# Four fused attention layers: the gates' loads moved a segment forward, a scale step, an update and two turns moved back on TensorE, and the first tiles' order rewritten

## The chip, the cores and the metric

The kernel runs on one NeuronCore of a Trainium2 chip. The metric is device time in microseconds (us) of one execution, as the median of several. Five engines work side by side, each through its own list of instructions in order: TensorE (PE in the profile; PEld is its weight loads), VectorE (DVE), ScalarE (ACT), GpSimd (POOL) and SyncE (SP, which here only issues DMAs).

## The reference

The input x has 2048 rows of 640 values; there are 32 heads of 20 values. Four layers follow each other, A, B, A, B, each on a normalized x and added to it, and both layers of a kind use the same weights.

```python
def _A_ref(x, wqkv, wo):                       # linear attention
    phi = lambda t: jnp.where(t > 0, t + 1, jnp.exp(t)) + 1e-6
    pq, pk = phi(q), phi(k)
    kv = jnp.einsum("bhsd,bhse->bhde", pk, v)
    z = jnp.einsum("bhsd->bhd", pk)
    num = jnp.einsum("bhqd,bhde->bhqe", pq, kv)
    den = jnp.einsum("bhqd,bhd->bhq", pq, z)[..., None] + 1e-6
    return (num / den) @ wo
def _B_ref(x, wq, wk, wv, wo, beta):           # 4 segments of 512 rows
    g = _sigmoid(beta).reshape(1, H, 1, 1)
    for s in range(N):
        p = _softmax(einsum("bhqd,bhkd->bhqk", qs, ks) * scale + mask)
        a_dot = jnp.einsum("bhqk,bhkd->bhqd", p, vs)
        num = jnp.einsum("bhld,bhde->bhle", phi(qs), M)
        den = jnp.einsum("bhld,bhd->bhl", phi(qs), z)[..., None] + 1e-6
        outs.append(g * num / den + (1.0 - g) * a_dot)
        M = M + jnp.einsum("bhld,bhle->bhde", phi(ks), vs)
        z = z + jnp.einsum("bhld->bhd", phi(ks))
x = x + _A_ref(_layernorm(x), ...); x = x + _B_ref(_layernorm(x), ...)   # twice
```

## The kernel before, in words

Rows are worked on in 4 segments of 512, each of 4 tiles of 128; the 640 columns are 5 chunks of 128. A value that TensorE multiplies is split in two fp16 parts, an upper half and a lower half (the rest), so that a product takes three matmuls per chunk: upper by upper, upper by lower, lower by upper. ACT writes upper halves, DVE lower ones, so almost each operand has an ACT step and a DVE step behind it.

**The opening** (`opening`, layer 1, up to about 260 us) prepares the eight weights while it computes the keys and queries of the first layer. `w_prep` prepares one: SP loads its five chunks into a stage (L239), DVE takes the largest magnitude of each (L243) and of these (L248), PE turns that column into a row with the identity (L252), DVE reduces the row (L254), PE spreads the one value to all partitions in a product with ones (L258: "the ones step"), DVE makes the scale of it (L261 to L264), ACT and DVE write the halves (L269, L270), and SP stores them (L275, wd). A turn (`turn`) is five transposes on PE (L329) whose result ACT and DVE copy as the halves of xT (L333, L334). Keys are products of xT with w_Ak (L406), then Exp and Relu on ACT (L418, L420), a sum on DVE (L421), and the halves pk (L556, L543). `memory` multiplies pk with xs, the normalized rows' halves (L487 on ACT, L488 on POOL, in `parts`), in products of L580, and DVE adds the results up (L602). At the end of segment 3 `merge` folds the memory with w_Av and w_Ao into one matrix wm: DVE takes reciprocals of the column sums (L646 to L648), scales the memory (L661), its halves are written (L663, L664), and PE multiplies them with w_Av (L682). `p_read` normalizes a tile of queries (pqi): POOL multiplies (L754, L760), DVE sums (rca, L757).

`gates` loads beta twice: as `gate`, 32 values on every partition (L205), and as `cg`, 8 columns on four rows, for which DVE first sets all to -10000 (L207) and SP issues four small loads (L209). Then ACT takes two Exps (L211, L212) and DVE adds one to each (L213, L214).

**The second phase** computes, layer by layer, queries times wm and the output (`a_head`, `a_second`), projects for the B layer (`b_project`), and runs B's attention beside it: scores (L993, L1034), maxima on DVE (L999), Exps on ACT (L1038), weighted sums (L1061). `b_project` also keeps the memory of layer B: for each of five chunks the keys' features pkT are turned by PE (L858), ACT copies the turn (pkt, L860), and `update` multiplies it with v (32 small matmuls, L868), which DVE adds to acc (L872 or L874). The last chunk's turn and update stand in `rest()`, which is woven with the next work, and its acc is masked to mem (L739), read by L457 a segment later.

**What sets the order.** PE's list is the order in which the code is written: parts of the work are generators, `weave` takes one step of the main one and a few of an auxiliary one in turn, and `pause(n)` lets n steps pass. On the other engines a scheduler orders the instructions by priority and readiness; `issue_after(x)` makes an instruction stand behind x, `high_priority` ahead of others. `busy(n)` issues n matmuls of the identity with itself (L320), whose result nobody reads.

## Time and profile before

| | |
|---|---|
| time, median of 3 runs | 1704.46 us (1704.25 to 1706.57) |
| profiled execution | 1704.55 us |
| its span, first to last instruction | 1702.8 us |
| mean granted TensorE clock | 0.992 |
| busy: PE, DVE, ACT, POOL | 96%, 75%, 58%, 30% of the span |

A row of the timeline gives the start, the time from there to the end of the last of its instructions, the engine, the line of the kernel, what is written and read, and how many instructions of a kind follow each other. In brackets stands how long the engine was idle ahead of it, and what ended that. SPq is SP's queue of DMA issues. A row of stretches gives, for each engine, the busy microseconds and the instructions, then the TensorE clock (1.00 is full speed), the share of time that the DMA engines were busy, and the rate.

### The profile page before, as it was taken

To read this page: it belongs to the slowest core of one execution; us is meant where nothing else is said; L and a number is where in the kernel's file an instruction comes from. 1 tells how busy PE (TensorE), PEld (TensorE's weight loads), DVE (VectorE), ACT (ScalarE), POOL (GpSimd) and SP (SyncE) were. 2 spreads that over 40 slices of the span, in tenths; PEclk is the share of its full clock that TensorE was granted. 3 is DMA by queue.
4 is the path that set the end of the run, shared out by engine and by line. 5 is a ranking of instruction groups with operands and counts; after the bars stand their busy time and mean duration, and the time that the engine had idled before them with its cause. 6 is when DMAs were issued, how large, how long until landed. Compare 5 with 4: busy or idle time off the path is not lost.

```text
span 1702.8 us, 37843 instructions
## 1 busy us (share of the span) xinstructions
PE 1637.9 (96%) x13788; PEld 1018.6 (60%) x13788; DVE 1272.3 (75%) x4015; ACT 994.2 (58%) x1888; POOL 505.9 (30%) x1046
## 2 busy tenths in 40 slices
PE   7999979999999999999999999999999999999998
PEld 5767757554465556556566777765546545645555
DVE  7888887487887788759874465847888978878773
ACT  6666533347756746667776454333675676666673
POOL 3442222013223322333452210310322332233452
PEclk9999989999999999999999999999999999999999
DMA  6424654421322331353211303423232323323432
GB/s 218 151 75 169 223 203 152 136 98 59 111 79 69 115 118 56 128 183 95 72 56 39 117 32 125 178 94 123 70 110 89 114 83 110 102 86 111 140 103 95
DMA packets 110372, 191.00 MB, mean 112 GB/s; under 512 B 14172, under 2 KB 69596, under 8 KB 107624
## 3 DMA queue, kind: packets, MB, share of 16 engines
q1 hardware_dynamic: 97704, 142.68, 25.9%
q0 software_dynamic: 3264, 24.91, 4.1%
q10 hardware_dynamic: 9216, 20.98, 3.2%
q8 instruction: 109, 1.79, 0.4%
q14 instruction: 79, 0.65, 0.1%
HBM read 109.32 MB, written 78.64 MB: 110 GB/s over the span
## 4 chain that ended last, share of the span: by engine, by line
PE 66%; DVE 17%; ACT 9%; issue 3%; DMA 3%; POOL 2%; SPq 0%; ACTq 0%; POOLq 0%; DVEq 0%
PE ps L406 25%; PE ps L391 13%; PE ps L1061 8%; PE ps L580 4%; PE ps L1034 4%; ACT pe L1038 3%; PE ps L993 3%; PE ps L329 3%; DVE ps L999 3%; PE ps L457 2%; PE ps L1074 1%; DVE e L421 1%; DVE wmx L243 1%; DVE split L270 1%; DVE xT L334 1%
## 5 line engine op out<-in xcount | busy, mean ns | idle before, releaser
L999 DVE CUSTOM_DVE_ANT_0 ps<-ps,maskw 128x512 f32<-128x512 f32 (+3 forms) x1024 | 472.0, 518 | 28.7 <-PE ps L993 25.9
L1038 ACT ACTIVATE pe<-ps,lsc 128x512 f32<-128x512 f32 x640 | 395.4, 696 | 63.0 <-PE ps L1034 59.8
L406 PEld LDWEIGHTS <-xT 128*128 128x128 f16 x2880 | 282.2, 99 | 115.0 <-issue 6.2
L1045 POOL TENSOR_SCALAR_AFFINE_SELECT pe<-pe 128x256 f32<-128x256 f32 (+1 forms) x640 | 233.4, 372 | 350.5 <-ACT pe L1038 342.7
L406 PEld LDWEIGHTS <-oT 128*128 128x128 f16 x1920 | 184.5, 98 | 84.7 <-issue 8.3
L1061 PE MATMUL ps<-pe,v 128*32 128x512 f32 (+3 forms) x2048 | 161.6, 436 | 8.8 <-DVE oT L334 1.9
L406 PE MATMUL ps<-wm,oT 128*128 128x320 f16 x960 | 141.3, 299 | 3.8 <-DVE rs L352 2.6
L406 PE MATMUL ps<-w_Bo,oT 128*128 128x320 f16 x960 | 141.5, 299 | 3.2 <-ACT oT L333 2.0
L406 PE MATMUL ps<-w_Ak,xT 128*128 128x320 f16 x960 | 140.6, 303 | 3.1 <-DVE xT L334 1.0
L406 PE MATMUL ps<-w_Bv,xT 128*128 128x320 f16 x960 | 142.3, 303 | 0.2
L391 PE MATMUL ps<-xT,w_Bq 128*128 128x512 f16 x600 | 140.9, 379 | 1.3 <-ACT pe L1038 0.8
L999 DVE DVE_READ_ACCUMULATOR2_ANT mg<- 128x1 f32 x1024 | 142.1, 139 | 0.1
L580 PE MATMUL ps<-pk,xs 128*128 128x321 f16 (+1 forms) x960 | 140.7, 304 | 1.1 <-DVE pk L543 0.7
L391 PE MATMUL ps<-xT,w_Bk 128*128 128x512 f16 x600 | 138.5, 379 | 1.2 <-ACT pe L1038 1.2
L406 PE MATMUL ps<-w_Aq,xT 128*128 128x320 f16 x960 | 137.6, 299 | 0.1
L993 PE MATMUL ps<-ks,qs 60*128 60x512 f16 (+3 forms) x1024 | 123.5, 297 | 7.6 <-ACT pe L1038 3.5
L580 PEld LDWEIGHTS <-xs 128*128 128x128 f16 x960 | 93.9, 99 | 41.0 <-issue 1.6
L421 DVE SCALAR_TENSOR_TENSOR e<-e,r 128x320 f32<-128x320 f32 x128 | 69.6, 544 | 53.6 <-ACT r L420 53.0
L1034 PE MATMUL ps<-qs,ks 62*128 62x512 f16 (+3 forms) x1024 | 105.6, 300 | 2.1 <-ACT pe L1038 1.1
L1061 PEld LDWEIGHTS ps<-pe,v 128*32 128x32 f32 x2048 | 65.4, 109 | 68.7 <-issue 40.9
L831 DVE SCALAR_TENSOR_TENSOR nat<-ps,nat 128x512 f16<-128x512 f32 x80 | 55.2, 690 | 62.6 <-ACT nat L830 62.3
L391 PEld LDWEIGHTS <-w_Bk 128*128 128x128 f16 x600 | 57.1, 98 | 66.5 <-issue 6.4
(202 smaller groups left out, 2359.6 us busy)
## 6 DMA issues: line engine op xcount, KB each, us to landing
x<-xn ACTq DMA_DIRECT2D x48, 320.0 KB
qs<-qd SPq DMA_DIRECT2D x128, 120.0 KB
ks<-kd SPq DMA_DIRECT2D x128, 120.0 KB
xo<-x SPq DMA_DIRECT2D x48, 320.0 KB
pqi<-pqd SPq DMA_DIRECT2D x32, 320.0 KB
qd<-nat SPq DMA_DIRECT2D x40, 256.0 KB
kd<-nat SPq DMA_DIRECT2D x40, 256.0 KB
x<-in_A_x SPq DMA_DIRECT2D x16, 320.0 KB
```

The costliest lines, as they stand in the source:

```text
L329: nc.tensor.transpose(pt[:, (c - c0) * P:(c - c0 + 1) * P], src[:, c * P:(c + 1) * P], self.ident)
L391: nc.tensor.matmul(p, w[:, c, a, t * P:(t + 1) * P], xT[:, c, b, :], start=k == 0, stop=k == 3 * C - 1)
L406: nc.tensor.matmul(p, xT[:, c, a, i * P:(i + 1) * P], w[:, c, b, n * HN:(n + 1) * HN], start=k == 0, stop=k == 3 * C - 1)
L421: nc.vector.scalar_tensor_tensor(e, e, 1.0, r, op0=OP.min, op1=OP.add)
L580: nc.tensor.matmul(p, xs[:, i, a, c * P:(c + 1) * P], pk[i][:, b, cols], start=i == 0 and a == b, stop=i == NT - 1 and a == 1)
L831: nc.vector.scalar_tensor_tensor(nat[:, 1], p, QK_SHIFT, nat[:, 0], op0=OP.mult, op1=OP.subtract)
L993: nc.tensor.matmul(bs[par][:, a:a + n], qs[r, p, i * P:(i + 1) * P], ks[r, p, :n], start=True, stop=True)
L999: nc.vector.tensor_tensor_reduce(bs[par][:, a:a + n], bs[par][:, a:a + n], self.maskw[:, SEG - n:], 1.0, NEG, OP.add, OP.max, G["mg"][:, p ...
L1034: nc.tensor.matmul(b[:, a:a + n], ks[r, p, j * P:(j + 1) * P], qs[r, p, j * P:], start=True, stop=True)
L1038: nc.scalar.activation(e, b, AF.Exp, scale=self.lsc)
L1045: nc.gpsimd.affine_select(d, d, pattern=pat, compare_op=OP.is_ge, fill=0.0, base=0, channel_multiplier=-1)
L1061: nc.tensor.matmul(G["pv"][32 * h4:32 * h4 + 32, j * P:], v[j][:, h * E1:h * E1 + 32], G.pop((p, par, j)), start=j == 0, stop=j == 2, skip ...
```

## The change

It has five parts.

1. `gates` is cut in two by a `yield`. Its loads and the setting of cg are taken in `late()`, an auxiliary step of segment 1, and the Exps and sums still in `last()`, in segment 3.
2. The ones step of weight A.v waits for 8 steps instead of 2.
3. The opening's first tiles: 11 identity products instead of 5 ahead of the first weight's maximum, 3 between its transpose and its ones step, 5 behind that in place of 3, and 4 behind the first two products. The first tile of keys takes its products in the order (0,0), (1,0), (0,1). `moments` is cut so that the second tile's shift (nb) stands behind six of the ten lower halves of w_Ak. The parts (xs) of a tile are queued behind the upper half of the next tile's turn.
4. In `p_read` the sum rca stands behind the last lower half of the merge's operand (L664).
5. `a_head` pauses two steps ahead of its turn in segments 1 to 3, and `rest()` one step between the keys' turn and the update.

In the core of the diff the first lines are parts 1 and 2:

```diff
+        yield 0.0
         nc.scalar.activation(g, g, AF.Exp, scale=-1.0)
         nc.scalar.activation(self.cg, self.cg, AF.Exp)
...
-        yield from pause(wait + 2 if key == ("A", "v") else wait)
+        yield from pause(wait + 8 if key == ("A", "v") else wait)
...
-            for a, b in ((0, 0), (0, 1), (1, 0)):
+            for a, b in ((0, 0), (1, 0), (0, 1)) if cold else ((0, 0), (0, 1), (1, 0)):
...
+                if cold and k == 2 and n == 0:
+                    self.busy(4)
...
-                nc.vector.tensor_tensor(t[:, c, 1, :HN], e, t[:, c, 0, :HN], op=OP.subtract)
+                L["parted"] = nc.vector.tensor_tensor(t[:, c, 1, :HN], e, t[:, c, 0, :HN], op=OP.subtract)
...
-        nc.vector.tensor_reduce(rc, q3, axis=AX.X, op=OP.add)
+        with self.tc.issue_after(L["parted"].ins):
+            nc.vector.tensor_reduce(rc, q3, axis=AX.X, op=OP.add)
...
+        yield from pause(2 if s else 0)
         yield from self.turn(box["o"][0], box["oT"][0], 0)
...
                 pk = pk_turn()
                 yield 440
+                yield from pause(1)
                 update(C - 1, pk)
...
         def late():
             self.setup_late(stage)
+            next(gates)
             yield 0.0
 
         def last():
             self.scales("B")
             with self.tc.issue_after(self.keyed.ins):
-                self.gates()
+                next(gates, None)
             yield 0.0
 
+        gates = self.gates()
...
-        self.busy(5)
+        self.busy(11)
         with self.tc.high_priority():
-            for _ in range(4):
+            for _ in range(3):
                 next(k)
             self.busy(3)
+            next(k)
+            self.busy(5)
             with self.tc.issue_after(self.last.ins):
-                m = self.moments(x[1])
+                m = self.moments(x[1], False)
             with self.tc.issue_after(self.taken.ins):
-                w("k")
+                for _ in range(5):
+                    next(k)
+            with self.tc.issue_after(self.last.ins):
+                m = self.shift(*m)
+            w("k")
...
-            with self.tc.issue_after((self.keyed or top).ins):
-                for i in range(NT):
-                    self.parts(xh[i], cur[2], i)
+                for j in range(i - 1, NT if i == NT - 1 else i):
+                    with self.tc.issue_after(self.upper.ins), self.tc.issue_after(top.ins):
+                        self.parts(xh[j], cur[2], j)
```

How the engines' lists move. First ACT in the opening, from the first tile's turn on, before (gate's Exp stands much further behind, after the keys of three tiles):

```order
L333 ACTIVATE xT<-ps 128x3x128
L333 ACTIVATE xT<-ps 128x2x128
L269 ACTIVATE w_Ak<-stage,scl_Ak 128x320 x10
L418 ACTIVATE e<-ps,inv_Ak 128x320
L420 ACTIVATE r<-ps,inv_Ak 128x320
L378 ACTIVATE xh<-x,nb,rs 128x640
L487 ACTIVATE xs<-xh 128x640
```

and now (lines behind L208 are one to twelve higher):

```order
L334 ACTIVATE xT<-ps 128x3x128
L334 ACTIVATE xT<-ps 128x2x128
L212 ACTIVATE gate<-gate 128x32
L270 ACTIVATE w_Ak<-stage,scl_Ak 128x320 x10
L424 ACTIVATE e<-ps,inv_Ak 128x320
L426 ACTIVATE r<-ps,inv_Ak 128x320
L382 ACTIVATE xh<-x,nb,rs 128x640
```

The Exp of gate moved ahead of w_Ak's upper halves; all that it waits for is gate's load. The xs that stood behind xh now stands behind the second tile's xT, and the Exp of cg follows it by a few rows. SP at the same place, before:

```order
L340 DMA x<-in_A_x 128x640 x3
L239 DMA stage<-in_A_wqkv 128x640 x5
L205 DMA gate<-in_B_beta 128x32
L275 DMA wd_Ak<-w_Ak 128x6400
L340 DMA x<-in_A_x 128x640 x4
```

and now:

```order
L341 DMA x<-in_A_x 128x640 x3
L240 DMA stage<-in_A_wqkv 128x640 x5
L205 DMA gate<-in_B_beta 128x32
L209 DMA cg<-in_B_beta 1x8x1 x4
L276 DMA wd_Ak<-w_Ak 128x6400
L341 DMA x<-in_A_x 128x640 x4
```

The load of gate was there already; the four of cg came from far behind, where they stood between the stores of B.k and of B.o. Further on, SP now stores A.o's halves ahead of B.v's stage loads, and no longer behind them. Second, DVE at the end of segment 3, ahead of the merge, before (L602 adds up the memory, L254 is the step of weight B.o that L258 on PE waits for):

```order
L207 MEMSET cg 128x8
L213 TENSOR_SCALAR gate<-gate 128x32
L421 SCALAR_TENSOR_TENSOR e<-e,r 128x320
L570 TENSOR_SCALAR e<-e 128x320
L602 TENSOR_TENSOR v_81<-ps,v_81 128x321
L659 TENSOR_SCALAR eps<-v_81,k_scl 128x1
L214 TENSOR_SCALAR cg<-cg 128x8
L602 TENSOR_TENSOR v_82<-ps,v_82 128x321
L254 TENSOR_REDUCE wm_2790<-ps 1x1
```

and now:

```order
L214 TENSOR_SCALAR gate<-gate 128x32
L215 TENSOR_SCALAR cg<-cg 128x8
L427 SCALAR_TENSOR_TENSOR e<-e,r 128x320
L576 TENSOR_SCALAR e<-e 128x320
L608 TENSOR_TENSOR v_81<-ps,v_81 128x321
L665 TENSOR_SCALAR eps<-v_81,k_scl 128x1
L608 TENSOR_TENSOR v_82<-ps,v_82 128x321
L255 TENSOR_REDUCE wm_2815<-ps 1x1
```

The sum of cg moved ahead of the last queries and memory sums; its setting went to the start of the program. Third, PE in segment 1, at the first memory products (with xs) behind the queries (w_Aq), before:

```order
L406 LDWEIGHTS xT
L406 MATMUL ps<-w_Aq,xT 128x320
L258 MATMUL ps<-wm_1386,ones 128x1
L580 LDWEIGHTS xs
L580 MATMUL ps<-pk,xs 128x321
```

Now the ones step of A.v stands behind 36 of the 120 products, and the transpose of A.o's maximum, which stood 24 products ahead of the end, stands at the end, right ahead of A.o's ones step:

```order
L586 LDWEIGHTS xs
L586 MATMUL ps<-pk,xs 128x320
L253 MATMUL ps<-ident,wm_1633 1x128
L259 MATMUL ps<-wm_1651,ones 128x1
L410 LDWEIGHTS xT
L410 MATMUL ps<-w_Ak,xT 128x320
```

In the second phase each of the six last updates (L868) moves behind 15 to 30 products and a few score matmuls, and each of the six turns of `a_head` in segments 1 to 3 behind 6 or more products with w_Bq.

More of the change, by code (lines that the diff above doesn't have):

```diff
@@ L332, in turn @@
             hi = dst[:, c0:c1, 0, i * P:(i + 1) * P]
-            nc.scalar.activation(hi, v, AF.Copy)
+            self.upper = nc.scalar.activation(hi, v, AF.Copy)
             self.lower = nc.vector.tensor_tensor(dst[:, c0:c1, 1, i * P:(i + 1) * P], v, hi, op=OP.subtract)
@@ L341, in load_x, with moments @@
         return x
-    def moments(self, x):
+    def moments(self, x, whole=True):
         nc, sb = self.nc, self.sb
@@ L353, in moments, with shift @@
         self.power = nc.gpsimd.tensor_tensor(rs, rs, self.mhalf, op=OP.pow)
-        nb = sb.tile([P, 1], F32, tag="nb", name="nb", bufs=4)
-        self.last = nc.vector.tensor_scalar(nb, mv[:, 0:1], rs, -1.0, op0=OP.mult, op1=OP.mult)
+        return self.shift(x, mv, rs) if whole else (x, mv, rs)
+    def shift(self, x, mv, rs):
+        nb = self.sb.tile([P, 1], F32, tag="nb", name="nb", bufs=4)
+        self.last = self.nc.vector.tensor_scalar(nb, mv[:, 0:1], rs, -1.0, op0=OP.mult, op1=OP.mult)
         return x, nb, rs
@@ L396, in proj_t, with proj_n @@
         return p
-    def proj_n(self, xT, w, i, n, p=None, cs=range(C)):
+    def proj_n(self, xT, w, i, n, p=None, cs=range(C), cold=False):
         nc = self.nc
@@ L554, in keys @@
                 z, c = slice(n * HN, (n + 1) * HN), slice(n * (HN + 1), n * (HN + 1) + HN)
-                e = self.phi_a(self.proj_n(xT, w("k"), i, n), self.inv["A", "k"])
+                e = self.phi_a(self.proj_n(xT, w("k"), i, n, cold=L["early"] and s == 0 and i == 0), self.inv["A", "k"])
                 nc.scalar.activation(pk[i][:, 0, c], e, AF.Copy, scale=self.k_scl)
```

## The prediction

> **What bounds the kernel now.** I read the page first, then PE's waits, then the timeline at the places that the change touches, then stretches with their granted clock. The page's busy times, and PE's 40 slices:

> ```profile
> PE 1637.9 (96%) x13788; PEld 1018.6 (60%) x13788; DVE 1272.3 (75%) x4015; ACT 994.2 (58%) x1888; POOL 505.9 (30%) x1046
> PE   7999979999999999999999999999999999999998
> ```

> TensorE is busy for 1637.9 of 1702.8 us, so nothing but its 65 us of idle time and its half-clock time can be won here; slices 0 and 5 hold much of it, and the change works in both. PE's list of waits (waiting line, what it waited for: sum, times, longest) names three rows that the change touches:

> ```profile
> PE ps L258 <- DVE wm L254: 8.1, 3, 5.6
> PE ps L868 <- ACT pkt L860: 2.3, 6, 0.4
> PE ps L329 <- POOL pqi L760: 1.1, 1, 1.1
> ```

> All sums are made against the profiled execution: 1704.55 us, of which 1702.8 are its span and 1.75 lie around it. The runs' median, 1704.46, is 0.09 lower, which I neglect. A measurement of this kernel tells about 0.2%, 3.4 us, from no change, so "faster" means below 1701.05 and "slower" above 1707.95.

> **Opening: +1.5.** The timeline of before (start, duration, engine, instruction, in brackets the idle time ahead of it):

> ```profile
> 8.19 1.28 PE L320 MATMUL ps<-ident 128*128 128x128 f32 x10
> 10.50 0.33 SPq L205 DMA_DIRECT2D gate<-in_B_beta  x1
> 12.73 4.63 ACT L269 ACTIVATE w_Ak<-stage,scl_Ak 128x320 f16<-128x320 f32 x10 [3.79 <-DVE scl_Ak L264]
> 14.95 4.24 DVE L270 SCALAR_TENSOR_TENSOR w_Ak<-stage,scl_Ak,w_Ak 128x320 f16<-128x320 f32 x9
> 18.67 0.53 ACT L418 ACTIVATE e<-ps,inv_Ak 128x320 f32<-128x320 f32 x1 [1.31 <-PE ps L406]
> 20.32 0.73 ACT L487 ACTIVATE xs<-xh 128x640 f16<-128x640 f32 x1
> 23.80 0.54 DVE L334 TENSOR_TENSOR xT<-ps,xT 128x384 f16<-128x384 f32 x1
> 24.40 1.94 PE L406 MATMUL ps<-w_Ak,xT 128*128 128x320 f16 x13 [1.00 <-DVE xT L334]
> 32.18 3.71 DVE L243 TENSOR_REDUCE wmx<-stage 128x1 f32<-128x640 f32 x5
> ```

> After the change the gate's Exp stands ahead of the ten upper halves of w_Ak on ACT (the rows of the order are in the section on the change), and it can only start when the gate's load has landed. When does it land? Three stretches (length, busy time of PE, PEld, DVE, ACT, POOL, then clock, DMA share, GB/s):

> ```profile
> 15.00:16.00 1.00, 0.83 (x4) 0.30 (x3) 1.00 (x4) 1.00 (x4) 0.00 (x0) 0.50 0.24 79
> 16.00:17.00 1.00, 1.00 (x5) 0.59 (x4) 1.00 (x3) 1.00 (x4) 0.00 (x0) 0.50 0.00 0
> 16.84:20.26 3.42, 3.42 (x14) 1.91 (x13) 3.42 (x9) 2.11 (x5) 0.00 (x0) 0.50 0.14 60
> ```

> The gate is the last of the opening's loads on SP, and the queues run dry only between 15 and 16 us. I take 16.4 for the landing, and with 0.2 for the Exp (as cg's at 223.50, below) the splits start at 16.6 in place of 12.73: ACT is held 3.9 us. What is left of that behind it: ten splits of 0.46 end at 21.2; the lower halves, now a run of ten at 4.24/9 = 0.47, end at about 22.0; the first Exp of keys starts at about 21.4 in place of 18.67, since its 1.31 us of waiting goes. From there ACT's chain is shorter than before by one xs (0.73), which goes behind tile 1's turn, and by part of a wait for products. Following the same instructions on ACT down to DVE's lower half of xT, tile 1's lower half comes at 25.25 instead of 23.80, and PE resumes near 25.85 instead of 24.40: +1.4. The reductions of the next weight (32.18) then start about 1.3 later, and their stage loads, queued behind a load that must now wait for POOL's later part, have under 1 us left; I take **+1.5**. The bounds: +3.9 if the hold passes on whole, -1.0 if the waits at 18.67 and 24.40 swallow it and the xs is won. The 15 more identity products (10 took 1.28 us at 8.19) lie where PE waits for DVE and ACT anyway: 0; without that cover, 15 x 0.13 = 1.9.

> **Segment 1, the ones step of A.v moved: +2.0.**

> ```profile
> 112.01 0.35 PE L258 MATMUL ps<-wm,ones 1*128 1x1 f32 x2 [1.79 <-DVE wm L254]
> 112.89 2.24 DVE L543 SCALAR_TENSOR_TENSOR pk<-e,k_scl,pk 128x320 f16<-128x320 f32 x1 [0.63 <-ACT pk L556]
> 115.19 11.89 PEld L580 LDWEIGHTS <-xs 128*128 128x128 f16 x86 [0.70 <-DVE pk L543]
> 127.25 0.27 PE L252 MATMUL ps<-ident,wm 128*1 128x128 f32 x1
> 127.86 0.27 DVE L254 TENSOR_REDUCE wm<-ps 1x1 f32<-1x128 f32 x1
> 130.73 0.38 PE L258 MATMUL ps<-wm,ones 1*128 1x1 f32 x2
> 132.47 3.38 SPq L239 DMA_DIRECT2D stage<-in_B_wv  x5
> 152.02 1.53 DVE L243 TENSOR_REDUCE wmx<-stage 128x1 f32<-128x640 f32 x2
> ```

> Two stretches of it, with the columns as above:

> ```profile
> 109.00:112.40 3.40, 1.61 (x13) 1.06 (x11) 3.23 (x5) 1.72 (x5) 2.39 (x3) 1.00 0.13 48
> 112.40:115.80 3.40, 3.29 (x13) 1.58 (x13) 2.64 (x2) 1.53 (x4) 2.47 (x4) 0.50 0.13 48
> ```

> The wait of 1.79 goes from L258, but ten memory products behind it then run at 110.3, and the eleventh needs the lower half of pk, which DVE finishes at 115.13 with or without the move: the end at 115.19 stays, and 1.79 + 0.70 become one wait of some 3.4. In before a stretch in which PE was busy 1.61 of 3.40 us was followed by one at clock 0.50. The longer wait leaves about 0.7 busy in the next such stretch, so 115.8 to 119.2, full now, goes to half: up to 1.7, and about 1.2 with the opening's shift, of which 0.3 comes back at 112.4. A.v's L258 itself (0.38) now stands between products, and A.o's L252 stands directly ahead of its L258, so that PE waits for DVE's L254 there: 0.7, since L254 ended 0.9 behind L252's start at 127.25, of which L252 itself is 0.27. Sum 1.2 - 0.3 + 0.4 + 0.7 = **+2.0**, bounds 0 (DVE done early) and +3.5. What is moved on SP with it, A.o's store ahead of B.v's stage loads, has cover: even 10 us later than at 132.47 they are issued 9.5 us ahead of their maxima at 152.02; without it, DVE would wait there one for one.

> [...]

> **Merge: -5.15.** The timeline around the gates and at the merge's end:

> ```profile
> 217.23 1.81 PE L580 MATMUL ps<-pk,xs 128*128 128x321 f16 x12
> 223.50 0.21 ACT L212 ACTIVATE cg<-cg 128x8 f32<-128x8 f32 x1 [6.59 <-DMA cg<-in_B_beta]
> 223.75 0.17 DVE L214 TENSOR_SCALAR cg<-cg 128x8 f32<-128x8 f32 x1 [5.14 <-ACT cg L212]
> 223.82 0.48 DVE L602 TENSOR_TENSOR v<-ps,v 128x321 f32<-128x321 f32 x1
> 224.64 0.55 PE L258 MATMUL ps<-wm,ones 1*128 1x1 f32 x2 [5.61 <-DVE wm L254]
> 247.34 0.80 DVE L757 TENSOR_REDUCE rca<-pqi 128x32 f32<-128x640 f32 x1
> 248.06 0.87 DVE L664 TENSOR_TENSOR xT<-ge,xT 128x320 f16<-128x320 f32 x2
> 248.59 4.06 PE L682 MATMUL ps<-xT,w_Av 128*128 128x80 f16 x35 [0.89 <-DVE xT L664]
> ```

> DVE's cg add waits 5.14 us for an Exp that waits for a load issued only at 216 us; PE's 5.61 at L258 is its consequence. With cg loaded in the opening both operands are there long before. What is late next is L602, which needs the twelve products that end at 219.04: it starts at about 219.25 in place of 223.82, so **-4.6**, and not 5.61. From there on DVE is the bound, with 24.85 of 25 us busy:

> ```profile
> 224.00:249.00 25.00, 21.62 (x175) 15.51 (x176) 24.85 (x53) 9.53 (x18) 6.43 (x11) 0.91 0.25 95
> ```

> So the shift arrives whole; the half clock behind the gap (mean 0.91) goes too, but PE isn't late there. The reduction of rca (0.80) stood ahead of the last two lower halves; behind them, they follow ACT's upper at about 247.5 in place of 248.06: **-0.55**. Bounds -4.1 (rca gains nothing and half a microsecond more is late) and -6.5 (all of 5.61, all of 0.89). In the second such merge, of layer 3, PE has no wait for L664, and I count nothing.

> **Pauses in the second phase: -1.3.**

> ```profile
> 344.50 0.65 PE L868 MATMUL ps<-v,pkt 128*32 128x63 f32 x32 [0.42 <-ACT pkt L860]
> 467.84 0.96 PE L457 MATMUL ps<-mem,pq 128*128 128x147 f32 x6
> 600.80 0.55 PE L329 MATMUL ps<-ident,pqi 128*128 128x128 f32 x3 [1.05 <-POOL pqi L760]
> ```

> and the stretch around the first of them:

> ```profile
> 336.00:372.00 36.00, 32.30 (x297) 21.30 (x296) 30.69 (x109) 14.39 (x28) 3.95 (x9) 1.00 0.35 117
> ```

> The pause of one step puts 15 products or more between the keys' turn and the update, so the six waits of 0.4 (2.3 in all) have their cover; the pause of two in a_head can take the 1.05. The result of the update at 344.50 is read as mem at 467.84, so it may come late. But in the stretch of the first of them DVE is busy 30.69 of 36 us while PE idles 3.7: there a wait removed tends to come back at the next row that needs DVE. Of 3.35 I take 1.3, about 40%; bounds -3.4 and, where oT comes late, +1.

> **Sum.** +1.5 + 2.0 - 5.15 - 1.3 = -2.95: 1704.55 - 2.95 = **1701.6**.

> **The rivals.**
> - Hold swallowed. The gate's wait costs nothing at the end of the opening (for: PE waits 1.00 at 24.40 anyway; against: DVE's splits start only behind ACT's). Opening -1.0: 1699.1.
> - Clock kept in segment 1, the term being +1.1 or less with the clock whole: 1700.7. For: the opening's shift changes the phase of the stretches. [...]
> - Hold passed on whole, +3.9: 1704.0.
> - Slower: the half clock spreads in the opening. PE has 0.50 in the three stretches from 15.00 to 20.26; if splits that come every 0.46 us keep it under half busy, every further stretch of 3.4 us costs up to 1.7. Hold 3.9 and three such stretches, 5.1, make +9.0: 1709.1. It decides from an opening 7.9 us longer. Against: at 0.50 PE was wholly busy from 16 to 20.26, and the clock then rose.
> - The edit on the gates doesn't do what it says: another late operand (a later cg Exp on ACT, pqi's loads) takes the place of the 5.14, and only rca's 0.55 is left: 1706.2.

> **How the numbers follow.** Forecast 0.40 (its own range 1699.5 to 1703.5; 0.16 of it below 1701.05, 0.24 above); hold swallowed 0.16 and clock kept 0.10, both faster; hold whole 0.17, same; slower rival 0.11; gates 0.06, of which 0.02 slower; and 0.03 of the hold's case, with B.v's loads late as well, slower. Faster 0.16 + 0.16 + 0.10 = 0.42; slower 0.11 + 0.02 + 0.03 = 0.16; same 0.42. The range, 1697.0 to 1707.0, takes in the bounds of the opening and of the pauses and leaves out most of the slower rival.

> **What would show it.** Right: ACT's w_Ak splits at about 16.6 with a wait on the gate's load; no wait on cg near 219; clock 0.50 behind 115 us. Wrong: splits still at 12.7; PE's L258 of B.o waiting over 1 us; a new wait of PE at L406 or L391 over 1 us behind the moved turns; or B.v's maxima waiting for their load.

## The result, and the profile after

The changed kernel takes 1708.48 us (median of 14 runs, 1704.42 to 1710.35), the kernel before 1704.51 (14 runs, 1700.92 to 1706.97). The ratio is 1.0021, 95% interval 1.0012 to 1.0029: 3.6 us slower, where the prediction had 2.9 faster. The profiled execution took 1706.88 us, 1705.2 of them its span. The page's first rows of after:

```profile
PE 1640.9 (96%) x13818; PEld 1021.3 (60%) x13818; DVE 1268.4 (74%) x4015; ACT 993.4 (58%) x1888; POOL 505.6 (30%) x1046
PE   8999999999999989999999999999999999999998
```

The two thin slices of PE, 0 and 5, are fuller, as the change meant them to be; slice 14 (597 to 639 us), where one of `a_head`'s turns was moved, went from 9 to 8. PE's longest waits have changed their names (line, what it waited for: sum, times, longest):

```profile
PE ps L1070 <- ACT pe L1047: 5.9, 7, 1.3
PE ps L866 <- DVE pkT L437: 4.1, 3, 2.7
PE ps L410 <- ACT w_Ak L270: 3.7, 1, 3.7
...
PE ps L586 <- DVE pk L549: 2.0, 1, 2.0
```

The 8.1 us at L258 are down to 1.0 (L259), and the 2.3 at L868 and the 1.1 at L329 are gone. In their place stand waits of the weighted sums (L1070) for ACT, of a turn (L866) for DVE, of the first products for w_Ak's split, and of memory products (L586) for pk. Where each costs time is seen when the two traces are laid side by side: the n-th ACT or DVE instruction of a kind in the one, and the n-th in the other, with the difference of their starts. A table of these differences (us behind the kernel before; negative is ahead):

```
at us of before     50   108   150   205   222   235   265   343   365   385   480   500   595   635   665  1172  1190  1310  1335  1448  1470  1690
after              1.9   1.4   3.5   3.3  -1.6  -0.6  -2.7  -2.7  -3.2  -4.6  -4.2  -3.1  -3.0  -2.2  -1.1  -1.1  -1.6  -1.5  -0.4  -0.5   0.6   2.0
```

So the kernel loses 3.3 us up to the merge, wins 6 there, and is 4.6 ahead at 385 us. Then it falls back by 0.4 at 440 us, 1.1 at 486, 0.8 at 606, 1.1 at 642, 1.1 at 1316, 1.1 at 1451 and 1.4 at 1647 us. The steps at 372 (-1.4) and 1647 (+1.4) are stretches of 3.41 us at half clock that the one trace has and the other hasn't, over the same instructions; the others are waits.

**The opening.** Rows of after's timeline:

```profile
11.15 0.33 SPq L205 DMA_DIRECT2D gate<-in_B_beta  x1
17.03 0.23 ACT L212 ACTIVATE gate<-gate 128x32 f32<-128x32 f32 x1 [7.81 <-DMA gate<-in_B_beta]
17.17 4.62 ACT L270 ACTIVATE w_Ak<-stage,scl_Ak 128x320 f16<-128x320 f32 x10
22.56 0.53 ACT L424 ACTIVATE e<-ps,inv_Ak 128x320 f32<-128x320 f32 x1 [0.77 <-PE ps L410]
26.66 1.94 PE L410 MATMUL ps<-w_Ak,xT 128*128 128x320 f16 x13 [0.23 <-DVE xT L335]
```

ACT waits for gate's load until 17.03, and the splits follow it: the forecast had the load at 16.4. It was issued 0.65 us later than in before (11.15 against 10.50), which is the difference.

**The second phase**, at the update of segment 1. First before, then after:

```profile
486.56 0.65 PE L868 MATMUL ps<-v,pkt 128*32 128x63 f32 x32 [0.36 <-ACT pkt L860]
488.24 0.92 ACT L378 ACTIVATE xh<-xn,nb,rs 128x640 f32<-128x640 f32 x1 [1.73 <-DVE nb L355]
489.77 1.26 ACT L1038 ACTIVATE pe<-ps,lsc 128x512 f32<-128x512 f32 x2 [0.24 <-PE ps L1034]
490.27 1.06 PE L1061 MATMUL ps<-pe,v 128*32 128x512 f32 x8 [0.15 <-DVE oT L334]
```

```profile
484.07 0.92 ACT L382 ACTIVATE xh<-xn,nb,rs 128x640 f32<-128x640 f32 x1 [1.73 <-DVE nb L359]
485.27 1.25 ACT L1047 ACTIVATE pe<-ps,lsc 128x512 f32<-128x512 f32 x2
486.09 1.07 PE L1070 MATMUL ps<-pe,v 128*32 128x512 f32 x8 [1.25 <-ACT pe L1047]
488.71 0.65 PE L876 MATMUL ps<-v,pkt 128*32 128x63 f32 x32
496.21 2.08 PE L410 MATMUL ps<-wm,oT 128*128 128x320 f16 x14 [0.32 <-DVE otok L1090]
```

The section on the change says that the update moves behind products and a few score matmuls. In segments 1 and 2 it also moves behind a group of weighted sums (32 matmuls of L1070), and the wait that grew stands ahead of these.

ACT's xh stands at 488.24 before and 484.07 after: 4.17 us apart, which is just the lead that the whole kernel has there. ACT's row of instructions is set by the normalization (nb), not by the update. PE's weighted sum, at 490.27 and 486.09, is 4.18 ahead too. PE arrives there earlier, by the update's 0.58 to the next product and its wait of 0.36, and waits 1.25 us in place of 0.15. The update now comes behind the sums, where PE has no wait that it could fill, and DVE's otok is late by 0.32 next. The work is the same, so the waits make the difference: 1.25 + 0.32 in place of 0.36 + 0.15 is 1.06, the step of 1.1 in the table.

The sum doesn't wait for the values of the Exp at that place. In before it starts at 490.27, 0.19 us ahead of that Exp's end (490.46); its operand is an older Exp. What it waits for is room: the results of matmuls go to eight banks that `bank()` hands out, and what a bank held must have been read before the sum may write to it. In the program of before the sum's bank held the turn, which ACT and then DVE copy to oT; in that of after, where the update takes its bank later, it held the scores that the Exp reads. Both stand behind xh on ACT, and in after they end at nearly the same time (DVE's oT at 485.96, the Exp at 485.95), so the old bank would have come free no earlier. It is so at all four places: in before each sum starts 0.19 us ahead of that Exp's end.

**The merge.** Rows of after:

```profile
219.75 0.16 DVE L215 TENSOR_SCALAR cg<-cg 128x8 f32<-128x8 f32 x1
222.25 0.48 DVE L608 TENSOR_TENSOR v<-ps,v 128x321 f32<-128x321 f32 x1
223.06 0.35 PE L259 MATMUL ps<-wm,ones 1*128 1x1 f32 x2 [0.30 <-DVE wm L255]
```

The add of cg waits for nothing, and PE waits 0.30 us at B.o's ones step where it waited 5.61.

### The profile page after: what moved, and what is told of

It is laid out like the page before. It is cut to its first block, busy times and chain, and to the rows that moved or that the text cites. A ratio compares the mean times of both kernels' runs of the same rounds, so it can differ in the third digit from the quotient of the medians.

```text
span 1705.2 us, 37896 instructions
## 1 busy us (share of the span) xinstructions
PE 1640.9 (96%) x13818; PEld 1021.3 (60%) x13818; DVE 1268.4 (74%) x4015; ACT 993.4 (58%) x1888; POOL 505.6 (30%) x1046
## 3 DMA queue, kind: packets, MB, share of 16 engines
q8 instruction: 109, 1.79, 0.5%
## 4 chain that ended last, share of the span: by engine, by line
PE 68%; DVE 15%; ACT 9%; DMA 3%; issue 3%; POOL 2%; SPq 1%; ACTq 0%; POOLq 0%; DVEq 0%
PE ps L410 27%; PE ps L395 13%; PE ps L1070 7%; PE ps L586 5%; PE ps L1043 4%; PE ps L1002 3%; PE ps L330 3%; ACT pe L1047 3%; DVE ps L1008 3%; PE ps L463 2%; PE ps L1083 1%; DVE e L427 1%; DMA x<-in_A_x 1%; DVE wmx L244 1%; DVE xT L335 1%
## 5 line engine op out<-in xcount | busy, mean ns | idle before, releaser
L1070 PE MATMUL ps<-pe,v 128*32 128x512 f32 (+3 forms) x2048 | 162.8, 436 | 13.0 <-ACT pe L1047 5.9
L586 PE MATMUL ps<-pk,xs 128*128 128x321 f16 (+1 forms) x960 | 139.3, 302 | 3.0 <-DVE pk L549 2.0
L586 PEld LDWEIGHTS <-xs 128*128 128x128 f16 x960 | 93.4, 98 | 42.0 <-DVE pk L549 2.5
L1070 PEld LDWEIGHTS ps<-pe,v 128*32 128x32 f32 x2048 | 65.6, 109 | 74.1 <-issue 46.3
```

The costliest lines, as they stand in the source:

```text
L586: nc.tensor.matmul(p, xs[:, i, a, c * P:(c + 1) * P], pk[i][:, b, cols], start=i == 0 and a == b, stop=i == NT - 1 and a == 1)
L1070: nc.tensor.matmul(G["pv"][32 * h4:32 * h4 + 32, j * P:], v[j][:, h * E1:h * E1 + 32], G.pop((p, par, j)), start=j == 0, stop=j == 2, skip ...
```

## The experiments

Two theories stood ahead of the first runs. **F**: the update had filled the time in which PE waits for the next Exp on ACT, and its move costs 1.1 us at four places. **S**: the loss is that of the opening and of segment 1 (3.3 to 3.7 us by 205 us), and the second phase only carries it. Beside them stood the question what each other part does alone.

Each kernel was timed against the kernel before on the same chip; microseconds are the ratio's excess over 1 times 1704.6. Line numbers are each kernel's own.

**1. The update at once.** The changed kernel without the pause in `rest()`.

```diff
                 yield 440
-                yield from pause(1)
                 update(C - 1, pk)
```

> The changed kernel without the pause between the last turn of keys and its update. Theory F (the update was what PE did while it waited for the next Exp; the trace of after is 1.1 us later behind each of the four updates at 486, 642, 1316 and 1451 us, and 0.5 earlier behind the two at 344 and 1175): the time falls by 4 x 1.1 - 2 x 0.5 = 3.4 us, to about 0.2 us over before, and the weighted sum (L1070) waits for ACT for at most 0.4 us behind the update. Theory S (the loss is that of the opening and of segment 1, 3.7 us by 205 us, and the second phase only carries it): the time stays at 3.6 us over before, within 1 us.

Ratio 1.0001 (0.9992 to 1.0009): 0.2 us over before, where the changed kernel is 3.6. The side-by-side trace is flat where after falls back (at 480 and 500 us -1.68 and -1.68, at 1310 and 1335 -0.51 and -0.50), and has no gain at 343 and 1172. Its rows at that update:

```profile
484.88 0.65 PE L876 MATMUL ps<-v,pkt 128*32 128x63 f32 x32 [0.36 <-ACT pkt L868]
488.59 1.07 PE L1069 MATMUL ps<-pe,v 128*32 128x512 f32 x8 [0.15 <-DVE oT L335]
```

Both waits of before are back, and together they are shorter than the one of after. Theory F holds, with the Exp as the end of the wait and not as the sum's operand.

**2. The Exps of the gates late.** The changed kernel, with both Exps behind a turn of segment 3 on ACT.

```diff
-            with self.tc.issue_after(self.keyed.ins):
+            with self.tc.issue_after(self.keyed.ins), self.tc.issue_after(self.upper.ins):
                 next(gates, None)
```

> The changed kernel with both Exps of the gates queued on ACT behind a turn of segment 3, the loads still early. If the hold of ACT at 17 us is what the opening costs (1.9 us behind at 44 us in the trace), the splits of w_Ak start at about 13.3 us, the opening is 1 to 2 us shorter and the time falls by as much, to 1.6 to 2.6 us over before. If the hold is hidden (rival), the shift at 44 us stays at 1.3 or more over before, and the time doesn't change. In both, the merge keeps its gain: no wait for cg near 219 us.

Ratio 0.9994 (0.9984 to 1.0005): 1.0 us under before, 4.6 better than the changed kernel. w_Ak's split starts at 13.30 in place of 17.17, and the trace is 0.7 us ahead of before at 50 us and 1.5 at 108, where after is 1.9 and 1.4 behind. The hold costs 2.6 to 2.9 us up to there in this pair of traces. At 205 us they are 4.6 apart: after has a stretch at half clock from 117.6 us, and this trace has none there.

**3. A.v's ones step back.** The changed kernel with the old pause.

```diff
-        yield from pause(wait + 8 if key == ("A", "v") else wait)
+        yield from pause(wait + 2 if key == ("A", "v") else wait)
```

> The changed kernel with the ones step of A.v where it was (pause of wait + 2). If the step of the prediction holds, the 2.1 us that the trace of after loses between 115 and 140 us do not arise: the shift against before stays within 0.5 us from 110 to 140 us, and the time falls by about 2 us, to 1.6 us over before. If that loss comes from the opening's shift (the phase of the clock's stretches) it stays, and the time with it.

Ratio 1.0015 (1.0005 to 1.0026): 2.6 us over before, 1 better than the changed kernel, with intervals that overlap. In the trace it is 2.4 behind at 150 us (after: 3.5), but 3.6 at 205 (after: 3.3): what was won at 150 is lost before the merge. Inconclusive for the time.

**4. a_head's turn at once.** The changed kernel without the other pause.

```diff
-        yield from pause(2 if s else 0)
         yield from self.turn(box["o"][0], box["oT"][0], 0)
```

> The changed kernel without the pause of two steps ahead of a_head's turn. In the trace of after the place at 600 to 615 us, where this turn stands, ends 0.8 us later than in before, and one at 440 us 0.4 later. If the turn's move makes that, the time falls by 1 to 2 us, to 1.6 to 2.6 over before. If the moved turn wins the wait of 1.05 us for POOL that before had at 601 us (prediction), the time rises by up to 1 us.

Ratio 1.0016 (1.0005 to 1.0026): 2.7 us over before, 0.9 better than the changed kernel, not clear of noise. In the trace the step of 0.8 at 606 us isn't there (0.09 at 595, 0.10 at 635). Its waits at that place, then the changed kernel's:

```profile
600.89 0.55 PE L330 MATMUL ps<-ident,pqi 128*128 128x128 f32 x3 [1.05 <-POOL pqi L767]
606.20 0.66 PE L865 MATMUL ps<-ident,pkT 128*128 128x128 f32 x4 [1.31 <-DVE pkT L437]
614.58 0.66 PE L865 MATMUL ps<-ident,pkT 128*128 128x128 f32 x4 [0.56 <-DVE pkT L437]
```

```profile
603.05 0.66 PE L866 MATMUL ps<-ident,pkT 128*128 128x128 f32 x4 [2.67 <-DVE pkT L437]
```

The 1.05 for POOL went, as predicted, and came back at the keys' turns: the wait of the first grew from 1.31 to 2.67, that of the next from 0.56 to 1.17 (at 612.25 in after). Together 3.84 stand in place of 2.92, and the 0.9 are the step of 0.8 in the table.

**5. The update late, alone.** The kernel before with that pause only.

```diff
                 yield 440
+                yield from pause(1)
                 update(C - 1, pk)
```

> The kernel before with nothing but the pause of one step between the last turn of keys and its update. Theory F (the update filled PE's wait for the next Exp): 1.1 us lost behind each of the four updates of segments 1 and 2, 0.5 won behind the two of segment 0: about 3.4 us slower than before. The prediction's step (the pause covers the wait for ACT's copy): 0.4 won at each of six, up to 2.3 us faster. A mixture with the opening as the cause (theory S): within 1 us of before.

Ratio 1.0023 (1.0014 to 1.0033): 3.9 us slower, by the pause alone. The trace falls back by 1.1 us at each of 486, 642, 1316 and 1451 us and wins 0.5 at 344 and 1175. Its waits of weighted sums for Exps, which summed to 0.9 in before:

```profile
PE ps L1062 <- ACT pe L1039: 5.9, 7, 1.3
```

The row is the same as after's, to the digit. Theory F is shown from both sides, by taking the pause out of the changed kernel and by putting it alone into the kernel before, and the prediction's step and theory S fall.

**6. The gates alone.** The kernel before with the loads in segment 1, the Exps held behind a turn of segment 3.

```diff
+        yield 0.0
         nc.scalar.activation(g, g, AF.Exp, scale=-1.0)
...
             self.setup_late(stage)
+            next(gates)
...
-            with self.tc.issue_after(self.keyed.ins):
-                self.gates()
+            with self.tc.issue_after(self.keyed.ins), self.tc.issue_after(self.upper.ins):
+                next(gates, None)
...
```

> The kernel before with the gates' loads in the second segment and their Exps held behind a turn of segment 3 on ACT, and nothing else. The prediction's step: DVE's wait of 5.14 us for cg goes and 4.6 us of it arrive behind the merge, so 4 to 5.5 us faster than before. Rival (another late operand takes its place): a new wait on DVE between 218 and 232 us and under 2 us won.

Ratio 0.9985 (0.9976 to 0.9994): 2.6 us faster, less than expected. In the trace 5.3 us are won between 205 and 222, and 1.0 is given back by 235: the lead is 4.7 at 343 us. The rows of before at the loss, and then of this kernel:

```profile
227.51 4.68 POOL L754 TENSOR_TENSOR pqi<-pqi,z 128x640 f32<-128x640 f32 x3 [7.86 <-DVE z L646]
231.71 1.29 DVE L661 SCALAR_TENSOR_TENSOR ge<-v,eps,rz 128x320 f32<-128x320 f32 x2
```

```profile
225.89 1.54 POOL L755 TENSOR_TENSOR pqi<-pqi,z 128x640 f32<-128x640 f32 x1 [1.05 <-DMA pqi<-pqd]
225.94 2.30 DVE L662 SCALAR_TENSOR_TENSOR ge<-v,eps,rz 128x320 f32<-128x320 f32 x2
```

The third tile of pqi hadn't landed yet, so POOL multiplies it later, beside DVE's two ge, and these take 2.30 us together in place of 1.29. After shows the same step (-1.6 to -0.6). Why the runs' 2.6 is less than the trace's 4.7 stays open; its interval (1.0 to 4.1) just touches the expected 4 to 5.5.

**7. Late Exps, and the pauses out where they cost.** The changed kernel with the late Exps (as in 2), no pause ahead of the turn (as in 4), and

```diff
-                yield from pause(1)
+                yield from pause(0 if s else 1)
                 update(C - 1, pk)
```

> The changed kernel with the Exps of the gates held behind a turn of segment 3, the pause ahead of the update in segment 0 alone, and none ahead of a_head's turn. If the terms add up (against the changed kernel: hold of ACT 2.6, four updates 4.4, turn 0.5), it is 7.5 us faster than the changed kernel and about 4 us faster than before. If they hide each other, it stays at the 0.5 to 1 us that the late Exps alone won over before.

Ratio 0.9959 (0.9947 to 0.9971): 7.0 us faster than before, 10.6 than the changed kernel. The interval is 4.9 to 9.0, and 1.0 (run 2) + 4.4 + 0.5 lies in it, so the terms add up within the noise. In the trace the lead of 5.2 us behind the merge is kept to the end (-5.7 at 1690).

**8. The opening alone, Exps late.** The kernel before with part 3 of the change, and

```diff
-            with self.tc.issue_after(self.keyed.ins):
+            with self.tc.issue_after(self.keyed.ins), self.tc.issue_after(self.upper.ins):
                 self.gates()
```

> The kernel before with only the opening's part of the change (identity products, order of products, split moments, parts behind the next turn), the gates loaded and computed as before but their Exps held behind a turn of segment 3 on ACT, so that the split of w_Ak isn't held. From the trace with late Exps (0.7 us ahead of before at 50 us, 1.5 at 85) it should be 0.7 to 1.5 us ahead at 200 us; whether it arrives is open: the wait for cg at 219 us ends with a load that is issued from DVE's setting of cg at 216 us, so it should move with the rest (0.7 to 1.5 us faster), unless that load's place sets the time (no change).

Ratio 0.9985 (0.9977 to 0.9994): 2.6 us faster. The trace is 3.2 ahead at 108 us and keeps 2.7. The stretches of the opening, of before, of after and then of this kernel (length, busy time of PE, PEld, DVE, ACT, POOL, clock, DMA share, GB/s):

```profile
10.02:13.43 3.41, 1.60 (x10) 1.22 (x11) 2.84 (x11) 0.70 (x2) 0.00 (x0) 1.00 1.04 407
13.43:16.84 3.41, 2.53 (x10) 1.10 (x10) 2.95 (x12) 3.41 (x9) 0.88 (x3) 0.50 0.53 193
```

```profile
10.02:13.43 3.41, 3.09 (x25) 2.69 (x25) 2.81 (x10) 0.00 (x0) 0.00 (x0) 1.00 1.04 409
13.43:16.84 3.41, 0.63 (x6) 0.46 (x5) 1.11 (x6) 0.00 (x0) 0.64 (x3) 1.00 0.56 202
16.84:20.26 3.42, 2.49 (x14) 1.98 (x14) 2.51 (x6) 3.23 (x8) 0.00 (x0) 0.75 0.00 0
```

```profile
10.02:13.43 3.41, 3.22 (x27) 2.82 (x26) 2.82 (x11) 0.34 (x1) 0.00 (x0) 1.00 1.04 405
13.43:16.84 3.41, 3.41 (x28) 2.62 (x27) 3.40 (x12) 3.41 (x9) 0.88 (x3) 1.00 0.56 205
16.84:20.26 3.42, 3.27 (x21) 1.81 (x19) 3.42 (x11) 3.38 (x8) 0.00 (x0) 1.00 0.16 65
```

With the identity products PE is busy 3.22 of 3.41 us ahead of the first products, and those then run at clock 1.00 throughout, where before, busy for 1.60, had 0.50 from 13.4 to 20.3. In after the clock stays at 1.00 past 16.84, but the products haven't begun: the hold leaves PE 0.63 us of work in that stretch, and from 18.6 to 22.0 the clock is 0.50, which makes the mean of 0.75. This isn't one trace's luck: the five kernels with the old opening (before and runs 5, 6, 10, 11) all have a half-clock stretch that begins between 12.1 and 14.9 us, and the four with part 3 and late Exps (2, 7, 8, 9) have none ahead of 21.9. The identity products weren't tried apart from the rest of part 3, so how much of the 2.6 us is theirs isn't shown.

**9. A.v's step put back as well.** Run 7's kernel with the diff of 3.

> The kernel of the run before last but one (late Exps, update paused in segment 0 alone, turn at once) with the ones step of A.v put back as well. If A.v's step costs 1.9 us for good (the trace of that run falls back from 2.3 to 0.2 us ahead of before between 118 and 150 us), it wins about 1.5 to 2 us more: 8.5 to 9 us faster than before. If the merge takes it back (the changed kernel with A.v's step alone undone was 1.5 us ahead of it at 150 us and 0.3 behind at 205), nothing is won: 7 us faster than before.

Ratio 0.9960 (0.9948 to 0.9972): 6.8 us faster than before, no different from run 7. The trace is 2.4 ahead at 150 us (run 7: 0.2) and 5.8 at 343 (run 7: 5.2).

**10. rca alone.** The kernel before with part 4.

```diff
-        nc.vector.tensor_reduce(rc, q3, axis=AX.X, op=OP.add)
+        with self.tc.issue_after(L["parted"].ins):
+            nc.vector.tensor_reduce(rc, q3, axis=AX.X, op=OP.add)
```

> The kernel before with nothing but the sum rca behind the merge's last lower half. The prediction's step: 0.55 us won at 248 us, none in layer 3. Rival: DVE has other work there and nothing is won. A gain over 1 us would say that the clock stretch behind it goes as well.

Ratio 0.9994 (0.9984 to 1.0003): not told from before. In the trace 0.5 us is won at 248 us (2.61 behind at 247, 2.11 at 249). The trace of this kernel was by then 2.6 behind, although its program is that of before up to there: 1.8 of it came between 118 and 150 us. It ran two stretches at half clock about there, and before one (112.4 to 115.8 us). So much can a single trace be off.

**11. A.v's step alone.** The kernel before with `wait + 8`.

> The kernel before with nothing but the ones step of A.v moved (pause of wait + 8). The prediction's step: 2.0 us lost between 110 and 150 us, half of it by a stretch at half clock near 116 us, and all of it still there at the end. Rival: lost there and given back by 205 us, so that the wait for cg or the queries hide it: within 0.5 us of before.

Ratio 1.0000 (0.9992 to 1.0009): no change. In the trace it loses 2.1 us by 150, still has 1.8 at 247, and 0.2 behind 265 us, where before has a stretch at half clock from 249 us that this trace lacks. Its waits:

```profile
112.88 0.31 PE L580 MATMUL ps<-pk,xs 128*128 128x321 f16 x1 [1.56 <-ACT pk L556]
115.15 5.41 PE L580 MATMUL ps<-pk,xs 128*128 128x321 f16 x26 [1.96 <-DVE pk L543]
...
133.21 0.38 PE L258 MATMUL ps<-wm,ones 1*128 1x1 f32 x2 [0.66 <-DVE wm L254]
```

All three are as the prediction had them: 1.56 + 1.96 = 3.5 in one place, and 0.66 new. The end of the wait, 115.15, is that of before (115.19).

**12. The opening as written.** Run 8's kernel without the late Exps, so with part 3 of the change alone.

> The kernel before with only the opening's part, as the change has it, so that gate's Exp stands ahead of w_Ak's split again. With late Exps this part was 3.2 us ahead of before at 108 us. If the hold passes on whole, 3.9 us, it is 0.7 behind at 108 us; with the changed kernel's own trace (1.4 behind at 108, of which 0.6 by a later landing of the first loads) 0.7 to 1.4 behind, and the time 0.7 to 1.4 us over before. If the hold is partly hidden, it stays ahead of before.

Ratio 1.0004 (0.9995 to 1.0013). Gate's Exp is held here too, though `gates` is as it was: it is part 3 that moved it ahead of w_Ak's split, and not part 1.

```profile
16.18 0.23 ACT L211 ACTIVATE gate<-gate 128x32 f32<-128x32 f32 x1 [7.07 <-DMA gate<-in_B_beta]
16.32 4.62 ACT L269 ACTIVATE w_Ak<-stage,scl_Ak 128x320 f16<-128x320 f32 x10
```

The trace is 1.2 behind at 108 us, run 8's 3.2 ahead: the hold is worth 4.4 us there, and 3.2 in the ratios (1.0004 less 0.9985).

## Why the prediction was wrong, point by point

- **Pauses in the second phase: wrong, and the step that decides.** Predicted -1.3, measured +3.9 for the update's pause alone (run 5), with about +0.9 for the turn's (run 4, unclear). The step that failed is "the six waits of 0.4 (2.3 in all) have their cover". They did get it: the row is gone. But I asked only what hides the wait, and not what the update itself was hiding: its 0.6 us and the wait of 0.4 ahead of it stood in the time until the next weighted sum may start, which ACT's chain sets. I gave the later position a bound of +1 "where oT comes late" and looked for harm in DVE and in mem's reader; the harm was one engine further, in ACT's chain. At 344 and 1175 us the same edit won 0.5 each, as forecast; at the four others it lost 1.1. Of the 6.5 us between forecast and result, 6.1 are this term (+4.8 in place of -1.3). None of the signs in the prediction watched the weighted sums: the three for "right" appeared, and none of those for "wrong".
- **Opening: +1.5 predicted, +0.7 measured (run 12, -0.9 to +2.2), 1.9 in the trace at 50 us.** The size was near, its make-up was not. That the number came near is luck. The hold isn't partly absorbed, as I had it: it costs 3.2 to 4.4 us, all of its 3.9 as far as the noise tells, and against it stand 2.6 us that the rest of part 3 wins (run 8), which I had at 1.0 at most. I had priced the 15 identity products at nothing, as filling waits; with them, though not shown to be by them alone, the first products ran at clock 1.00 (run 8) where before had 0.50. Their price without cover was wrong too: ten rows of 1.28 us are five products of two rows each, so fifteen last 3.8 us and not 1.9 (after has just 30 PE instructions more than before).
- **Segment 1: +2.0 predicted; +2.1 in the trace at 150 us, 0.0 in the time** (run 11, -1.4 to +1.5). Place and waits came as forecast. So did the half clock in after (0.51 from 117.6 to 121.0), but that is chance in part: of the six traces with this move, four have a half-clock stretch that begins between 112 and 118 us and two (runs 1 and 2) have none; of the eight without it, three have one. That the 2.0 us last to the end isn't shown: run 3 loses as much again by 205 us, and run 11 makes it good at 249. What gives it back is open; the stretches at half clock fall differently in each trace and hide it.
- **Merge: -5.15 predicted.** In after's trace -4.85 by 222 us, +1.0 by 235, and -2.1 from there to 265: -6.0. Of the last 2.1, 0.5 is rca's (run 10), and the rest goes with a stretch at half clock that before has at 249 us. The term for rca was right, and cg's too at its place. In the time the gates alone win only 2.6 (run 6, 1.0 to 4.1). What the prediction lacked is the step at 235: with a lead of 5 us pqi's load is late, and DVE takes 1.0 us longer beside POOL's later product. That accounts for 1.0 of what is missing; the rest is open.
- **Sum.** With the update's 3.9, the turn's 0.9, the gates' -2.6, rca's -1.0, the opening's 0.7 and A.v's 0.0, the parts measured alone make +1.9 against 3.6 (2.0 to 4.9) for the whole. Each part has an interval of 1 to 1.5 us to either side, so they agree, but what the remaining 1.7 is isn't known. Apart from the pauses the terms missed by -0.8 (opening), -2.0 (segment 1) and +1.6 (merge), and these misses nearly cancel.
- **The rivals.** None of the five names the update. The third had the hold right (passed on whole), but not what the rest of part 3 wins against it. The one on the slower side, the half clock spreading over three more stretches of the opening, didn't come: after has one such stretch there.

The clock in segment 1. In after the stretch before 117.6 us had PE busy 1.29 of 3.40 us, with no wait over 1.96, and the next ran at 0.51; in before 1.61 of 3.40 us were followed by 0.50. The half-clock stretches of these two traces last 3.41 us or twice that, and within a trace they begin whole multiples of 3.41 us apart (before at 13.43, 112.42, 221.65, 248.95, 371.83 and 1201.27 us; after at 18.57, 117.56, 240.44, 1199.58 and 1646.73). What makes the clock fall isn't shown. After's two stretches at 117.6 us, and PE's two waits in the first of them:

```profile
114.20:117.60 3.40, 1.29 (x8) 0.80 (x9) 2.64 (x3) 1.53 (x5) 2.50 (x3) 0.99 0.13 48
117.60:121.01 3.41, 3.41 (x15) 1.95 (x13) 3.06 (x7) 1.63 (x4) 1.49 (x3) 0.51 0.07 28
```

```profile
114.35 0.31 PE L586 MATMUL ps<-pk,xs 128*128 128x321 f16 x1 [0.98 <-ACT pk L562]
116.62 1.74 PE L586 MATMUL ps<-pk,xs 128*128 128x321 f16 x9 [1.96 <-DVE pk L549]
```

## What to carry to other kernels

Before an instruction is moved out of a wait, ask what it was covering where it stood: a 0.4 us wait ahead of 0.65 us of work may be the cheapest place for both, when the engine's next real wait ends at a time that another engine sets. Then list all that the moved instruction passes, and read what the first wait behind its old place waits for: it can be room for a result, and not an operand. A scheduler may move an instruction that the diff doesn't touch (gate's Exp went ahead of the first split because of an edit to the split), so compare each engine's order, and tie a helper that waits for a late load behind something on its own engine. A change of several parts that comes out flat or slow should be taken apart: here the gates and the opening win 2.6 us each once the Exps are late, rca and A.v's step can't be told from nothing, and one pause loses 3.9. With late Exps, no pause ahead of the turn and the update's pause in segment 0 alone, the kernel is 7.0 us faster than before.
